# Loading the first gate block as two whole halves, with all three parameter rows moved to GpSimd, in a one-core scan-and-gate kernel

## The chip, the cores and the metric

The kernel runs on one core of one Trainium2 chip. The metric is the device time of one execution in microseconds (us). The kernel before takes 183.2 us, the median of three runs (183.2 to 183.42).

## What is computed

The reference normalises a sequence x of 2048 tokens by 448 channels, and sends the result through two branches. Branch A is a diagonal complex state-space scan over the tokens; branch B is a gated two-layer block whose inner width is 1792. The output is x plus the product of A with silu(B).

```python
x = A_x                                    # (1, 2048, 448) bf16
xn = layernorm(x)
# A: Lam_bar = exp(dt*Lam); h_t = Lam_bar*h_(t-1) + B_bar xn_t ; s = 2 Re(C h) + xn*Dskip
# B: h = sigmoid(xn @ w_gate) * (xn @ w_up) ; b = h @ w_down   (w_gate, w_up: 448 x 1792)
return x + s * silu(b)
```

## The kernel before

The 2048 tokens are cut into 16 tiles of 128 and four chunks (c = 0 to 3) of four tiles. For each chunk TensorE (PE) computes 14 blocks of 128 columns of the gate and of the up product (lines 808 and 809), the projection of branch A (`b_phase`, lines 882 to 899), and later the down product (line 1024) and the output of A (line 1043). ScalarE (ACT) applies tanh to the gate blocks (lines 842 and 839), VectorE (DVE) multiplies by the up blocks (line 845) and runs the scan (line 963), GpSimd (POOL) does small arithmetic, SyncE (SP) issues nearly all DMAs.

A planner, `Plan`, decides the order. Every operation is given to it with an engine, a cost and its reads and writes; `solve` first gives each operation a due time counted back from PE's fixed order, then simulates forward and, on each engine, picks the ready operation that is due first. A DMA's landing is modelled from a rate and, if `land` is given, is not earlier than that. The order that comes out is then issued as it is: each engine works through its own list and waits at the head of it. So the numbers `land` change no transfer, but they decide which instruction stands ahead of which on ACT, DVE and POOL.

PE's product of a block of 128 columns needs two halves of weights, on the lower and the upper 64 partitions (line 808 reads the one, line 809 the other). The gate weights come in three blocks of columns: m = 0 and 1, m = 2 and 3, m = 4 to 6. Before, the first block comes in four pieces, A and B of each half (`load_w0`, lines 374 to 379): piece A holds the row groups that PE's first products on tile 0 read (part "b" of `last_tile`, lines 826 and 827), piece B the rest (part "a"). Three pieces are issued by SP and one by ACT. The three parameter rows (`load_p`, line 400) go one by SP and two by POOL; they are transposed on PE by `columns` (lines 635 and 637), which stands in PE's order between the transposes of tile 0 and the first product. A memset by POOL of two elements of the second gate block (line 418) makes SP's later weight loads wait for POOL. Every DMA on SP or ACT also uses one of eight semaphores in turn, and its issue waits until the DMA eight places earlier has landed.

At the start PE runs ten warming products (line 445), transposes tile 0 (lines 569 and 571), the parameter rows, part "b" of tile 0, the transposes of tile 1 (lines 589 and 590), part "a" of tile 0, then the rest. Tiles 0 to 3 are normalised by DVE (line 531). Tiles 4 to 7 follow for the next chunk: statistics by DVE (lines 451 and 457), a power by POOL (lines 510 and 511), two small operations by DVE (lines 513 and 514, tile `nmr`), then the normalisation by ACT (line 535). Sine and cosine tables are made by DVE (lines 676, 678 and 688) and ACT (lines 669, 681, 683 and 685). Three PSUM tiles `gu` are used in turn by PE's products; u5, the sixth up block of chunk 0, and the second part of `b_phase` of chunk 0 share one of them.

Of the kernel before, what the change touches and what calls it, by code (L numbers as in the profile page):

```python
# [14 lines left out]
ACT = mybir.ActivationFunctionType  # L15
# [3 lines left out]
D = 448  # L19
F = 1792  # L20
P = 128
H = 64
# [51 lines left out]
class Plan:  # L74
# [10 lines left out]
    def add(self, eng, cost, fn, r=(), w=(), dma=0, lat=None, chain=False, name="", rate=230e3):  # L85
        o = Op()
        o.idx, o.eng, o.cost, o.fn, o.dma, o.name = len(self.ops), eng, cost, fn, dma, name
        o.lat = LAT.get(eng, 0.0) if lat is None else lat
        o.pre, o.suc, o.rate = {}, [], rate
        o.slot, o.land = None, 0.0  # L90
        if dma and eng != "POOL":
            o.slot, self.n_dma = self.n_dma, self.n_dma + 1
        o.start = o.end = None
        for k in r:
            if k in self.w:
                self._edge(self.w[k], o, True)
        for k in w:
            for q in self.r.get(k, ()):
                self._edge(q, o, False)
            if k in self.w:  # L100
                self._edge(self.w[k], o, True)
        for k in w:
            self.w[k] = o
            self.r[k] = []
        for k in r:
            if k not in w:
                self.r.setdefault(k, []).append(o)
        if chain or eng == "PE" or (eng in ("DVE", "ACT") and self.seq):
# [138 lines left out]
def kernel(  # L247
# [18 lines left out]
    V, A, G, T, Q = nc.vector, nc.scalar, nc.gpsimd, nc.tensor, nc.sync  # L266
# [17 lines left out]
    wgt = {"g": sbt("wG", [7, 896]), "u": sbt("wU", [7, 896])}  # L284
# [66 lines left out]
    add = pl.add  # L351
# [3 lines left out]
    def load(eng, key, nbytes, o, i, cost=0.45, r=(), rate=230e3, land=0.0):  # L355
        e = {"SP": Q, "ACT": A, "POOL": G}[eng]
        add(eng, cost, lambda: e.dma_start(out=o, in_=i), w=[key] if not isinstance(key, list) else key,  # L357
            r=r, dma=nbytes, chain=True, rate=rate).land = land

    def load_x(t0, n, q="SP", r=(), rate=230e3, land=0.0):  # L360
        load(q, [("x", t) for t in range(t0, t0 + n)], n * P * D * 2,
             x_all[:, t0:t0 + n, :], x_src[:, t0:t0 + n, :], r=r, rate=rate, land=land)
# [8 lines left out]
             wgt[k][ps, :, m0 * P:m1 * P],  # L371
             wsrc[k][:, c0 + m0 * P:c0 + m1 * P].rearrange("(s p) f -> p s f", p=H), cost=0.65, r=r, rate=rate, land=land)

    def load_w0(eng, half, part, r=(), land=0.0):
        ps = slice(half * H, half * H + H)
        s0, c0 = (1 - half if part == "A" else half), half * 896
        n = 4 - s0
        load(eng, [("w", "g", half, m, part) for m in range(2)], H * n * 2 * P * 2, wgt["g"][ps, s0:7:2, 0:2 * P],
             wsrc["g"][:, c0:c0 + 2 * P].rearrange("(s p) f -> p s f", p=H)[:, s0:7:2, :], cost=0.5, r=r, rate=400e3, land=land)

    def wkeys(k, m, part=None):
        if k == "u" or m > 1:
            return [("w", k, 0, m), ("w", k, 1, m)]
        if part == "b":
            return [("w", k, 0, m, "A"), ("w", k, 1, m, "A")]
        return [("w", k, h, m, q) for h in range(2) for q in "AB"]

    def load_wd(h):
        fs = slice(h * 7, h * 7 + 7)
# [11 lines left out]
    def load_p(eng, k, r=()):  # L401
        load(eng, ("vrow", k), D * 2, vrow[k:k + 1, :], (A_log_dt, A_Lambda_im, A_Lambda_re)[k].unsqueeze(0), cost=0.75 if eng == "POOL" else 0.45, r=r)
    load_x(0, 1, "SP")
    load_x(1, 1, "ACT")
    load_x(2, 1, "SP", rate=180e3)
    load_x(3, 1, "ACT", rate=180e3)
    load_p("SP", 2)
    add("ACT", 0.05, lambda: A.preload_act_table_set("sqrt_and_others"), w=["sqrttab"], lat=1.3, chain=True)
    load_w0("SP", 0, "A", land=5.7)
    load_w0("ACT", 1, "A", land=5.9)  # L410
    load_w0("SP", 0, "B", land=6.9)
    load_w0("SP", 1, "B", r=[("x", 1)], land=6.9)
    load_p("POOL", 0)
    load_p("POOL", 1)
    add("POOL", 0.15, lambda: G.memset(ident[:], 0.0), w=["ident"], chain=True)
    add("POOL", 0.4, lambda: G.affine_select(out=ident[:], in_=ident[:], compare_op=ALU.not_equal, fill=1.0, base=0,
                                             pattern=[[-1, P]], channel_multiplier=1), r=["ident"], w=["ident"], chain=True)
    add("POOL", 0.1, lambda: G.memset(wgt["g"][0:1, 0, 256:258], 0.0), w=[("w", "g", 0, m) for m in (2, 3)], chain=True)
    load_w("SP", "g", 0, 1, rate=400e3, land=8.8)
    load_w("SP", "g", 1, 1, rate=400e3, land=9.8)  # L420
    load_w("SP", "g", 0, 2, rate=400e3, land=11.2)
    load_w("SP", "g", 1, 2, rate=400e3, land=12.6)
    load_x(4, 2, land=14.0)
    add("POOL", 0.1, lambda: G.memset(halfc[:], 0.5), w=["consts"])
    add("POOL", 0.1, lambda: G.memset(negc[:], -1.0), r=["consts"], w=["consts"])
    add("POOL", 0.1, lambda: G.memset(expc[:], math.e), w=["expc"])
# [3 lines left out]
                                    allow_small_or_imprecise_dtypes=True), w=[("wv", 0)])  # L430
    add("POOL", 0.15, lambda: G.memset(flat(g_raw[:, 512:2048], 3, 512)[:, :, D:512], 0.0),
        w=[("xnw", t) for t in (1, 2, 3)])
    load_w("SP", "u", 0, 0, rate=400e3, land=15.6)
    load_w("SP", "u", 1, 0, rate=400e3, land=16.8)
    load_x(6, 2, land=17.9)
    load_w("SP", "u", 0, 1, rate=400e3, land=19.0)
    load_w("SP", "u", 1, 1, rate=400e3, land=20.1)
    load_w("SP", "u", 0, 2, rate=400e3, land=21.6)
    load_w("SP", "u", 1, 2, rate=400e3, land=23.1)


    def warm_mm(n, w=512):
# [299 lines left out]

    def b_load():
        for i, m in enumerate((A_B_re, A_B_im)):
            tload([("bT", i)], bT[:, 0:3, i, :], m[:, 0:384], D * 768, land=25.0 + 1.7 * i)
            tload([("bT3", i)], bT[:, 3:4, i, :], m[:, 320:448], D * 256, land=25.7 + 2.0 * i)
# [68 lines left out]
    def last_tile(c, k, steps, j, hs="ba"):  # L815
        x, w_ = xnT[c % 3], wgt[k]
        ts = slice(j * P, j * P + P)
        for h in hs:
            ss = {"a": (0, 2, 4, 6), "b": (1, 3, 5), "c": (0, 2, 4), 1: (6,)}[h]
            for m, a in steps:  # L820
                ms = slice(m * P, m * P + P)

                def f(ms=ms, a=a, ss=ss):
                    for s in ss:
                        go, end = (s == 1, s == 6) if hs[0] == "b" or hs == "a" else (s == 0, s == 5)
                        T.matmul(gu[a][:, 0, ts], lhsT=w_[0:H, s, ms], rhs=x[0:H, SL[s], ts], start=go, stop=end)  # L826
                        T.matmul(gu[a][:, 1, ts], lhsT=w_[H:P, (s + 1) % 7, ms], rhs=x[H:P, SL[s], ts], start=go, stop=end)  # L827
                add("PE", len(ss) * 0.0562, f, r=[("xnT", c % 3, j, "a" if h == "c" else h)] + wkeys(k, m, "b" if h == "b" else "a"), w=[("gu", a)],
                    name=f"{k}{c}.{m}")

    sg_n = [0]
# [227 lines left out]
    def yout(c, j, first=False):  # L1059
        t = c * TPC + j  # L1060
        g, o, q = gt_of[c, j], next_o(), t % NXD
        a = next_acc()
        key, ok, od = ("acc", a), ("o", o, 0), o_t[o][:]
        y = y_mm(c, j, acc[a], key, 0, D, False, first)
        add("DVE", dve1(D), lambda: V.tensor_tensor(out=od, in0=y, in1=xd[q][:], op=ALU.add), r=[key, ("xd", q)], w=[ok])
        add("DVE", dve2(D), lambda: V.tensor_tensor(out=od, in0=od, in1=g_t[g][:], op=ALU.mult), r=[ok, ("gt", g)], w=[ok])
        add("DVE", dve2(D), lambda: V.tensor_tensor(out=od, in0=od, in1=x_all[:, t, :], op=ALU.add), r=[ok, ("x", t)], w=[ok])
        rows = (0, H, P) if c == 2 and j == 3 else (0, P)
        for r0, r1 in zip(rows, rows[1:]):
            store(t, od, 0, D, r0, r1, [ok])  # L1070

# [84 lines left out]
    gu_mm(0, "g", 3, None, 0, TPC, False)  # L1156
    gu_evac(0, "g", 3, None)
    b_load()
    load("SP", "dbc", P * D * 2, dbc[:], A_Dskip.unsqueeze(0).to_broadcast((P, D)), rate=400e3, land=29.0)

    def stats_for(c):
        for t in range(4 * c, 4 * c + 4):
# [103 lines left out]
```

## Time and profile before

| What | Value |
|---|---|
| median of three runs | 183.2 us |
| span of the profiled execution, first to last instruction | 181.5 us |
| granted TensorE clock | 1.000 |
| busy: PE, DVE, ACT, POOL | 177.1, 166.4, 98.2, 37.6 us |
| first four x tiles, issue to landing | 2.4 to 2.9 us |
| first gate block, last piece: issued, landed | 3.47, 7.21 us |
| x tiles 4 and 5: issued, landed | 6.86, about 13.7 us |
| x tiles 6 and 7: issued, landed | 8.84, about 17.3 us |

The profiled execution's own time beside its span is not listed; the median stands 1.7 us over the span, which is what lies around it. "Landed" is the issue's start plus the time to landing that the trace gives for that DMA; for the last piece of the gate block it is the end of its entry in the chain. The profile's engine rows count busy time; a matmul is pipelined, so that a start-to-start distance says more than a duration. Times in the chain and the timeline count from the first instruction.

### The profile page before, as it was taken

The page shows a single profiled execution, that of the slowest core. Times are in us where ns is not written, and L with a number is a line of the kernel's source. Part 1 is how long each engine was busy: PE and PEld are TensorE (multiplying, and loading weights), DVE is VectorE, ACT ScalarE, POOL GpSimd, SP SyncE. Part 2 cuts the span into 40 slices and gives each one's busy share as a digit, 9 for nine tenths or more (in the row PEclk, how much of TensorE's full clock was granted, in tenths as well). Part 3 has the DMA queues.
Part 4 walks back from the last instruction along what each step waited for, and adds up shares of the span by engine and source line. Part 5 has one row for each costly group of instructions (what it writes and reads, how often), then busy time and mean ns, then how long its engine had stood idle before and what let it go on. Part 6 is the DMA issues. An engine that isn't in the chain of part 4 may idle for free.

```text
span 181.5 us, 3611 instructions
## 1 busy us (share of the span) xinstructions
PE 177.1 (98%) x1404; PEld 88.2 (49%) x1411; DVE 166.4 (92%) x294; ACT 98.2 (54%) x162; POOL 37.6 (21%) x94
## 2 busy tenths in 40 slices
PE   8999999999999999999999999999999999999993
PEld 2664445664544444445554444444555444455552
DVE  3778799999989999999999999999999999999772
ACT  5799998857699985364155543348110533411100
POOL 6472468100018797000004100000000000000000
PEclk9999999999999999999999999999999999999999
DMA  5999999999000290000004900002000000002121
GB/s 133 227 224 229 160 165 207 252 242 257 23 0 0 52 148 6 0 4 0 0 2 88 143 0 0 4 0 69 7 4 0 25 27 28 1 0 76 47 65 47
DMA packets 30853, 13.43 MB, mean 74 GB/s; under 512 B 19442, under 2 KB 30835, under 8 KB 30835
## 3 DMA queue, kind: packets, MB, share of 16 engines
q1 hardware_dynamic: 30210, 12.83, 34.9%
q10 hardware_dynamic: 560, 0.36, 0.7%
q8 instruction: 11, 0.18, 0.5%
q14 instruction: 8, 0.06, 0.1%
q0 software_dynamic: 64, 0.00, 0.0%
HBM read 6.77 MB, written 1.84 MB: 47 GB/s over the span
## 4 chain that ended last, share of the span: by engine, by line
PE 94%; DMA 2%; SPq 1%; DVE 1%; issue 0%; DVEq 0%
PE gu L808 43%; PE gu L1024 15%; PE acc L1043 11%; PE acc L1024 9%; PE gu L896 8%; DMA wG<-in_B_w_gate_dram 2%; PE acc L899 2%; PE gu L882 2%; SPq L357 1%; PE gu L826 1%; PE acc L808 1%; PE gu L809 1%; DVE o_t L1085 0%; PE gu L827 0%; DVE o_t L1079 0%
## 5 line engine op out<-in xcount | busy, mean ns | idle before, releaser
L808 PE MATMUL gu<-xnT,wU 64*128 64x512 bf16 x196 | 45.8, 376 | 0.0
L809 PE MATMUL gu<-xnT,wU 64*128 64x512 bf16 x196 | 45.8, 376 | 0.0
L808 PE MATMUL gu<-xnT,wG 64*128 64x512 bf16 (+1 forms) x189 | 41.3, 360 | 0.0
L809 PE MATMUL gu<-xnT,wG 64*128 64x512 bf16 (+1 forms) x189 | 41.3, 360 | 0.0
L842 ACT ACTIVATE sig<-gu 128x1024 f32<-128x1024 f32 x21 | 21.3, 1019 | 24.4 <-PE gu L809 19.8
L1024 PEld LDWEIGHTS <-hF 128*128 128x128 bf16 x224 | 21.9, 98 | 20.6
L808 PEld LDWEIGHTS <-wU 64*128 64x128 bf16 x196 | 18.4, 94 | 22.9
L808 PEld LDWEIGHTS <-wG 64*128 64x128 bf16 x196 | 18.4, 94 | 19.9
L1024 PE MATMUL gu<-wd,hF 128*128 128x448 bf16 x140 | 28.0, 352 | 0.0
L845 DVE SCALAR_TENSOR_TENSOR hF<-sig,gu 128x1024 bf16<-128x1024 f32 x21 | 25.4, 1210 | 0.7 <-ACT sig L842 0.4
L1043 PE MATMUL acc<-cT,hT 128*128 128x448 bf16 (+2 forms) x119 | 22.9, 337 | 0.0
L963 DVE TENSOR_TENSOR_SCAN wv<-c_r,st,z 128x512 bf16<-128x512 f32 x18 | 22.8, 1273 | 0.0
L1030 ACT ACTIVATE g_t<-gu 128x448 bf16<-128x448 f32 x10 | 5.4, 540 | 27.7 <-PE gu L1024 16.8
L809 PEld LDWEIGHTS <-wU 64*128 64x128 bf16 x196 | 18.4, 94 | 0.0
L809 PEld LDWEIGHTS <-wG 64*128 64x128 bf16 x196 | 18.4, 94 | 0.0
L1024 PE MATMUL acc<-wd,hF 128*128 128x448 bf16 x84 | 16.9, 352 | 0.0
L1043 PEld LDWEIGHTS <-hT 128*128 128x128 bf16 x126 | 11.7, 98 | 9.9 <-issue 0.4
L896 PE MATMUL gu<-xnT,bT 128*128 128x512 bf16 x65 | 15.3, 379 | 0.4
L910 ACT CAST bus<-gu 128x1024 bf16<-128x1024 f32 x12 | 12.0, 1011 | 5.9 <-PE gu L882 5.3
L541 POOL COPY xn<-xn 128x448 bf16<-128x448 bf16 x12 | 7.5, 627 | 27.2 <-ACT xn L535 27.0
L916 ACT CAST bus<-acc 64x256 bf16<-64x256 f32 (+1 forms) x24 | 8.7, 368 | 4.8 <-PE acc L899 4.5
L535 ACT ACTIVATE xn<-x_all,nmr,rsd 128x448 bf16<-128x448 bf16 x12 | 8.8, 758 | 3.7 <-DVE xd L546 2.2
(162 smaller groups left out, 263.1 us busy)
## 6 DMA issues: line engine op xcount, KB each, us to landing
wd<-in_B_w_down_dram SPq DMA_DIRECT2D x2, 784.0 KB, 6.6
out_dram<-o_t SPq DMA_DIRECT2D x14, 112.0 KB, 1.7
wU<-in_B_w_up_dram SPq DMA_DIRECT2D x4, 224.0 KB, 8.4
x_all<-in_A_x_dram SPq DMA_DIRECT2D x2, 448.0 KB, 5.0
wG<-in_B_w_gate_dram SPq DMA_DIRECT2D x2, 336.0 KB, 5.4
wU<-in_B_w_up_dram SPq DMA_DIRECT2D x2, 336.0 KB, 8.5
wG<-in_B_w_gate_dram SPq DMA_DIRECT2D x2, 224.0 KB, 4.1
x_all<-in_A_x_dram SPq DMA_DIRECT2D x2, 224.0 KB, 7.7
```

Source lines behind the costliest of these rows:

```text
L535: add("ACT", 0.65, lambda: A.activation(o[:, 0:448], x_all[:, t, :], ACT.Identity, bias=nmr[:, t, :], scale=rsd[:, t, :]), r=[("x", t), (" ...
L541: add("POOL", 0.25 if n == H else 0.6, lambda: G.tensor_copy(out=o[:, D:D + n], in_=o[:, 0:n]), r=[("xn", b)], w=[("xnw", b)])
L808: T.matmul(bank[0][:, ts], lhsT=w_[0:H, s, ms], rhs=x[0:H, SL[s], ts], start=(s == 0), stop=(s == 6))
L809: T.matmul(bank[1][:, ts], lhsT=w_[H:P, (s + 1) % 7, ms], rhs=x[H:P, SL[s], ts], start=(s == 0), stop=(s == 6))
L842: add("ACT", act(1024), lambda: A.activation(th, gu[a][:], ACT.Tanh, scale=0.5), r=[("gu", a)], w=[tk])
L845: add("DVE", dve1(1024), lambda: V.scalar_tensor_tensor(out=ho, in0=th, scalar=1.0, in1=gu[a][:], op0=ALU.add, op1=ALU.mult), r=[("gu", a) ...
L896: T.matmul(gu[slots[pt]][:, i, :], lhsT=bT[:, kt, i, pt * P:pt * P + P], rhs=x[:, kt, :], start=(first and kt == 0), stop=(not first and k ...
L910: add("ACT", act(1024), lambda: A.copy(out=bus[u][:], in_=gu[slots[pt]][:]), r=key(pt), w=[("bus", u)])
L916: add("ACT", 0.36, lambda ns=ns, d=d, q=q, l=l, i=i: A.copy(out=bus[u][d, l, ns], in_=acc[a3[i]][q, 0:256]), r=[("acc", a3[i])] + ([("bus" ...
L963: dve(1.194, lambda k=k: V.tensor_tensor_scan(out=wv[:, k, :], data0=rb, data1=z[:, k, :], initial=(st[pt][:, k, :] if c else 0.0), op0=AL ...
L1024: T.matmul(d, lhsT=hF[c % 2][:, m, h, js], rhs=wd[:, ft, :], start=(ft == 0), stop=(ft == FT - 1))
L1043: T.matmul(y, lhsT=hT[c % 2][:, hm, js], rhs=cT[:, cm, c0:c1], start=(i == 0 and not skip_on_pe), stop=(i == 6))
```

## The change

The first gate block is loaded as two whole halves with the helper that the later blocks use, one half by SP and one by ACT. The third parameter row is issued by POOL, behind the other two. The two-element memset goes, so that SP's list runs x, x, first block, second block, third block, x tiles 4 and 5, the up weights with x tiles 6 and 7 in between. Nearly all `land` numbers of the planner get smaller. The output rows of the four tiles of chunk 2 are each stored in two halves of 64 rows, where only the last of them was.

The order of instructions on PE stays the same. On DVE, the statistics of tiles 4 to 7 move ahead of table operations, and those of tiles 6 and 7 now stand ahead of the `nmr` operation of tiles 4 and 5; the skip rows of two tiles stand ahead of one line-845 operation. On ACT, the normalisation of tile 4 (line 535) now stands ahead of the tanh of the seventh gate block, and those of tiles 5 and 6 ahead of the tanh of the fourth. On POOL, one bias copy of the B matrix stands ahead of the copy of tile 7.

```diff
-    def load_w0(eng, half, part, r=(), land=0.0):
...
-    def wkeys(k, m, part=None):
-        if k == "u" or m > 1:
-            return [("w", k, 0, m), ("w", k, 1, m)]
-        if part == "b":
-            return [("w", k, 0, m, "A"), ("w", k, 1, m, "A")]
-        return [("w", k, h, m, q) for h in range(2) for q in "AB"]
+    def wkeys(k, m):
+        return [("w", k, 0, m), ("w", k, 1, m)]
...
-    load_x(2, 1, "SP", rate=180e3)
-    load_x(3, 1, "ACT", rate=180e3)
-    load_p("SP", 2)
+    load_x(2, 1, "SP", land=3.7)
+    load_x(3, 1, "ACT", land=3.8)
+    load_w("SP", "g", 0, 0, rate=400e3, land=5.4)
     add("ACT", 0.05, lambda: A.preload_act_table_set("sqrt_and_others"), w=["sqrttab"], lat=1.3, chain=True)
-    load_w0("SP", 0, "A", land=5.7)
-    load_w0("ACT", 1, "A", land=5.9)
-    load_w0("SP", 0, "B", land=6.9)
-    load_w0("SP", 1, "B", r=[("x", 1)], land=6.9)
+    load_w("ACT", "g", 1, 0, rate=400e3, land=5.4)
+    load_w("SP", "g", 0, 1, rate=400e3, land=6.7)
+    load_w("SP", "g", 1, 1, rate=400e3, land=7.3)
     load_p("POOL", 0)
     load_p("POOL", 1)
+    load_p("POOL", 2)
...
-    add("POOL", 0.1, lambda: G.memset(wgt["g"][0:1, 0, 256:258], 0.0), w=[("w", "g", 0, m) for m in (2, 3)], chain=True)
-    load_w("SP", "g", 0, 1, rate=400e3, land=8.8)
-    load_w("SP", "g", 1, 1, rate=400e3, land=9.8)
-    load_w("SP", "g", 0, 2, rate=400e3, land=11.2)
-    load_w("SP", "g", 1, 2, rate=400e3, land=12.6)
-    load_x(4, 2, land=14.0)
+    load_w("SP", "g", 0, 2, rate=400e3, land=8.5)
+    load_w("SP", "g", 1, 2, rate=400e3, land=9.9)
+    load_x(4, 2, land=10.9)
...
-    load_x(6, 2, land=17.9)
+    load_x(6, 2, land=14.2)
...
-        rows = (0, H, P) if c == 2 and j == 3 else (0, P)
+        rows = (0, H, P) if c == 2 and j > -1 else (0, P)
```

The `land` numbers of the up weights, of the B matrix and of the skip row are lowered in the same way (the last up half from 23.1 to 19.4).

More of the change, by code (lines that the diff above doesn't have):

```diff
@@ L372, in load_w @@
              wsrc[k][:, c0 + m0 * P:c0 + m1 * P].rearrange("(s p) f -> p s f", p=H), cost=0.65, r=r, rate=rate, land=land)
-    def load_w0(eng, half, part, r=(), land=0.0):
[L375 to L379, printed above, removed]
-    def wkeys(k, m, part=None):
-        if k == "u" or m > 1:
-            return [("w", k, 0, m), ("w", k, 1, m)]
-        if part == "b":
-            return [("w", k, 0, m, "A"), ("w", k, 1, m, "A")]
-        return [("w", k, h, m, q) for h in range(2) for q in "AB"]
+    def wkeys(k, m):
+        return [("w", k, 0, m), ("w", k, 1, m)]
     def load_wd(h):
@@ L432 @@
         w=[("xnw", t) for t in (1, 2, 3)])
-    load_w("SP", "u", 0, 0, rate=400e3, land=15.6)
-    load_w("SP", "u", 1, 0, rate=400e3, land=16.8)
-    load_x(6, 2, land=17.9)
[L436 to L439, printed above, removed]
+    load_w("SP", "u", 0, 0, rate=400e3, land=12.0)
+    load_w("SP", "u", 1, 0, rate=400e3, land=13.0)
+    load_x(6, 2, land=14.2)
+    load_w("SP", "u", 0, 1, rate=400e3, land=15.2)
+    load_w("SP", "u", 1, 1, rate=400e3, land=16.2)
+    load_w("SP", "u", 0, 2, rate=400e3, land=17.8)
+    load_w("SP", "u", 1, 2, rate=400e3, land=19.4)
     def warm_mm(n, w=512):
@@ L744, in b_load @@
         for i, m in enumerate((A_B_re, A_B_im)):
-            tload([("bT", i)], bT[:, 0:3, i, :], m[:, 0:384], D * 768, land=25.0 + 1.7 * i)
-            tload([("bT3", i)], bT[:, 3:4, i, :], m[:, 320:448], D * 256, land=25.7 + 2.0 * i)
+            tload([("bT", i)], bT[:, 0:3, i, :], m[:, 0:384], D * 768, land=22.0 + 2.0 * i)
+            tload([("bT3", i)], bT[:, 3:4, i, :], m[:, 320:448], D * 256, land=22.6 + 2.0 * i)
             add("POOL", 0.7, lambda i=i: G.tensor_copy(out=bT6[:, 0:3, i * H:i * H + H], in_=bT[:, 0:3, i, 384:448]),
@@ L827, in f @@
                         T.matmul(gu[a][:, 1, ts], lhsT=w_[H:P, (s + 1) % 7, ms], rhs=x[H:P, SL[s], ts], start=go, stop=end)
-                add("PE", len(ss) * 0.0562, f, r=[("xnT", c % 3, j, "a" if h == "c" else h)] + wkeys(k, m, "b" if h == "b" else "a"), w=[("gu", a)],
+                add("PE", len(ss) * 0.0562, f, r=[("xnT", c % 3, j, "a" if h == "c" else h)] + wkeys(k, m), w=[("gu", a)],
                     name=f"{k}{c}.{m}")
@@ L1158 @@
     b_load()
-    load("SP", "dbc", P * D * 2, dbc[:], A_Dskip.unsqueeze(0).to_broadcast((P, D)), rate=400e3, land=29.0)
+    load("SP", "dbc", P * D * 2, dbc[:], A_Dskip.unsqueeze(0).to_broadcast((P, D)), rate=400e3, land=26.0)
     def stats_for(c):
```

## The prediction

> **What bounds the kernel.** I read the page first: PE is busy 98% of the span, and the chain that ended last is PE for 94% of it.
>
> ```profile
> span 181.5 us, 3611 instructions
> ...
> PE 177.1 (98%) x1404; PEld 88.2 (49%) x1411; DVE 166.4 (92%) x294; ACT 98.2 (54%) x162; POOL 37.6 (21%) x94
> ...
> PE 94%; DMA 2%; SPq 1%; DVE 1%; issue 0%; DVEq 0%
> ```
>
> The kernel ends when PE ends, plus a tail of DVE and one store. So the change can win only where PE stands still, and it touches PE only in the first 30 us. There the chain, in order of time, runs through SP's issues into one transfer:
>
> ```profile
> 2.02 0.75 SPq L357
> ...
> 2.81 0.61 SPq L357
> ...
> 3.47 3.74 DMA wG<-in_B_w_gate_dram
> ...
> 7.25 0.23 PE gu L827
> ```
>
> The fourth piece of the first gate block, issued at 3.47, lands at 7.21 and lets PE go on. The timeline around it shows how much PE lost:
>
> ```profile
> 6.73 0.22 PE L590 MATMUL gu<-ident,g_t 128*128 128x128 bf16 x1
> ...
> 6.88 0.23 PE L826 MATMUL gu<-xnT,wG 64*128 64x128 bf16 x1
> ...
> 7.25 0.09 PEld L827 LDWEIGHTS <-wG 64*128 64x128 bf16 x1 [0.28 <-DMA wG<-in_B_w_gate_dram]
> ```
>
> Line 827 follows line 826 by 0.37 us; further on the two start together (7.32 and 7.32). So the stall is **0.37 us**, and from 7.25 to the end PE's groups show no idle time but 0.4 us in all at line 896, without a releaser. This is the most the change can give: 0.2% of the time. A difference of 0.2% is also about what a measurement of this kernel can tell from no change.
>
> **What the change does, part by part.**
>
> *The first block.* Now all 448 KB of it must be there for PE's first product (6.11 in the timeline), where before piece A of both halves sufficed (landed 2.02 + 4.0 = 6.0 and 1.69 + 4.2 = 5.9). When does it land? I take the DMA columns of half-microsecond windows (share, then GB/s):
>
> ```profile
> 2.50:3.00 0.50, 0.50 (x3) 0.22 (x2) 0.00 (x0) 0.44 (x1) 0.42 (x3) 1.00 1.03 307
> 3.00:3.50 0.50, 0.50 (x3) 0.15 (x2) 0.39 (x1) 0.22 (x1) 0.50 (x6) 1.00 0.95 288
> 3.50:4.00 0.50, 0.50 (x2) 0.15 (x1) 0.47 (x3) 0.45 (x2) 0.50 (x4) 1.00 0.58 106
> 4.00:4.50 0.50, 0.50 (x2) 0.15 (x1) 0.50 (x2) 0.44 (x2) 0.06 (x2) 1.00 0.76 171
> ...
> 5.50:6.00 0.50, 0.50 (x10) 0.33 (x7) 0.43 (x4) 0.44 (x3) 0.00 (x0) 1.00 0.56 125
> ```
>
> Until 3.5 the windows have moved (84+242+307+288) x 0.5 = 460 kB, which is the four x tiles (4 x 112 KB). Then the engines run half empty, because the pieces were issued late. In the changed kernel SP issues its half right behind x (at 1.64, where the parameter row stood, some 0.65 each) and ACT at 1.69, both done by 2.4. The remaining 459 kB then go from 3.5 on, at a rate between 177 GB/s (mean of the six windows 3.5 to 6.5) and 297 (mean of 2.5 to 3.5): 1.55 to 2.6 us. To landing I add 0.6 (the fourth x tile landed at 1.19 + 2.9 = 4.1 with its bytes moved by 3.5). That is 5.65 to 6.7. I take **5.65**, since both queues will be loaded as in 2.5 to 3.5, the nearest row. Then PE starts at 6.11 as before, held by ACT's copy of tile 0, and the stall is gone: **-0.37**. Landing at 6.7 would start PE at 6.75, and part "a" 0.77 later (6.88 - 6.11) at 7.52 instead of 7.25: +0.27. Break-even is 6.45.
>
> Behind the stall, what is late next? The transposes of tile 3 need DVE's normalisation, ending at 6.88 + 0.40 = 7.28; moved 0.37 forward they start at 7.67. Part "b" of tile 1 needs a DVE copy ending at 8.21; PE reaches it near 8.42. Both hold. The second gate block is needed at 10.34 instead of 10.71 and landed at 4.84 + 4.3 = 9.1; it now comes earlier.
>
> A rule of the Trainium skill speaks against one half of the idea: DMA: Bandwidth & Descriptors, section "Issuing engines are not separate DMA queues", says that DMAs from several engines share the same 16 DMA engines, and that a second issuing engine saves only issue time. The windows agree: 277 to 300 GB/s at 6.5 to 7.5, with SP's queue alone, against 288 to 307 with both. By it the gain is from the earlier issue alone, which is how the sum counts it.
>
> *The parameter rows.* POOL's two rows were issued at 1.25 and 2.02 and took 3.0 and 2.9 us. The third follows at 2.53 and lands near 5.45 (bounds: 4.9, where the second landed, and 6.0, with another half us of crowding). `columns` on PE starts at 5.69 and has about 0.05 us of cover before part "b" at 6.11, so cost 0, or up to 0.3 at the late end. POOL's setup moves 0.5 us later: `epsc` ends at 3.7, needed by ACT at 4.06; the rest ends near 4.6, and POOL was idle until 5.10. The memset saves 0.1 there.
>
> *ACT, DVE and the x tiles.* Here a new bound stands. ACT's list is dense from 8.2 to 30 us, and PE's `b_phase` hangs on it:
>
> ```profile
> 25.14 0.61 ACT L683 ACTIVATE spm<-hT 128x512 bf16<-128x512 f32 x1
> ...
> 25.79 0.68 DVE L688 TENSOR_SCALAR spm<-spm 128x512 bf16<-128x512 bf16 x1
> ...
> 27.72 2.55 DVE L845 SCALAR_TENSOR_TENSOR hF<-hF,gu 128x1024 bf16<-128x1024 bf16 x2
> ...
> 28.84 0.59 PE L882 MATMUL gu<-xnT,bT 64*128 64x512 bf16 x4
> ```
>
> The sine table ends at 25.75 on ACT, DVE takes it at 25.79 and works without a break until u5 is out at about 28.95; the second pair of line 882 needs that PSUM tile at about 29.05. So PE can come forward there only as far as ACT does, plus 0.08. How far does ACT come? Its scaling at 9.19 waits for POOL (8.71 + 0.23), so it gains 0.14 only; the tanh of the sixth block at 16.96 waited for PE 0.12 and starts at 16.70; the next item is free at 17.62. One idle of 0.15 (before 21.83) falls away too. From there to 25.14 is the same work in another order, so the table starts at 24.71: 0.43 earlier, which with 0.08 covers 0.37. But the next item is now tile 4's normalisation, which waits for `nmr` of tiles 4 and 5, and that waits on DVE behind the statistics of tiles 6 and 7. From the landing of x 6 and 7 it is 1.35 us of statistics (17.58 to 18.93 before), and about 0.55 for lines 513, 676 and 514: landing + 1.9. (DVE is free for them by then: x 4 and 5 at 12.2, and 3.2 of statistics and table work behind them.) On time means a landing by **15.7**; each us later costs PE a us. Before it landed at 17.3. All loads keep their order, so they ride on the first block: if that is done 7.21 - 5.65 = 1.55 us earlier, x 6 and 7 land at 15.8. The bound there is 0.51 - 0.1 = 0.41, and 0.37 passes. The other end (first block at 6.7) puts them at 16.8: 0.51 - 1.1 = -0.6.
>
> *The stores.* Three more issues for SP, of 0.33 to 0.6 us, between items it waits for (61.8 us of waiting for line 1067). A half took 2.7 us to land against 1.7; output tile (3,1) is written at 173.08, and its buffer's last half would be issued near 169.5 and land near 172.2. Cost 0; if late, DVE's 1.55 us of idleness before 177.63 covers it.
>
> **Sum.** 181.5 - 0.37 = 181.1 of span, and with 1.7 around it 182.85; the median shown is 183.2, so I predict **182.85 us**.
>
> **Rivals.**
> 1. *The x tiles hold ACT* (slower). DVE's statistics of tiles 6 and 7 now stand ahead of what ACT waits for. It decides above a landing of 16.2, where ACT's 0.51 is spent. For it: landings before lagged further behind with every load. Against: SP issues those tiles some 2 us earlier. At 16.8: 183.8; at the old 17.3: 184.3. Chance 0.18.
> 2. *The block lands between 6.1 and 6.45, or x between 15.8 and 16.2*: the stall is partly kept, 182.9 to 183.3. Chance 0.20.
> 3. *The block or the third row lands late*, since all of it is now needed at once and POOL's row shares the engines with more traffic: block at 6.7, 183.5; row at 6.0, 0.3 lost of 0.37, 183.1. For it: the slow windows from 3.5 may be the transfers' own start, not late issue. Chance 0.12.
>
> **How the numbers follow.** Forecast 0.50, with its own range 182.75 to 182.95: the limit of 0.37 lies just at the 0.2% (182.83), so about half of it counts as faster. Faster: 0.26. Slower by over 0.2% (above 183.57): rival 1 nearly whole and some of 3, 0.25. Within: 0.49. Range: 182.7 to 183.8 leaves out the worse part of rival 1 and little else.
>
> **What would show it.** Right: no idle before line 827 of old, PE's first 512-column product at about 10.35 instead of 10.71, the second pair of `b_phase` near 28.7. Wrong: an idle on PE before part "b" named after wG or the row; ACT idle before tile 4's normalisation near 17.6 with DVE waiting for x; PE idle at about 29 behind DVE.

## The result, and the profile after

The changed kernel takes **185.07 us** (median of six executions, 183.97 to 186.63) against 183.2 (182.94 to 183.42) beside it on the same chip: a ratio of 1.0114, 95% interval 1.0072 to 1.0157. It is slower by 1.9 us between the medians; the ratio, here and below, is that of the means. The six fall into two groups: three at 183.97 to 184.37, with a granted TensorE clock of 1.000, and three at 185.77 to 186.63, with 0.988 to 0.991. The median lies between the two. The profiled execution is of the first group: 184.29 us, span 182.5.

The page of the changed kernel: the tensor engine (PE) is as busy as before, and the chain that ended last is still nearly all PE, but its DMA share rose from 2% to 3%.

```profile
span 182.5 us, 3621 instructions
...
PE 94%; DMA 3%; DVE 1%; ACTq 0%; issue 0%; ACT 0%; DVEq 0%
```

The chain of work in order of time (start, duration, what) now has ScalarE's (ACT's) half of the first gate block where SyncE's (SP's) fourth piece stood:

```profile
0.73 0.41 ACTq L357
1.17 0.46 ACTq L357
1.69 5.71 DMA wG<-in_B_w_gate_dram
```

That half was issued 1.8 us earlier than the piece that PE waited for before, and it landed at 1.69 + 5.71 = 7.40, 0.2 us later than that piece (7.21). The timeline of PE (start, duration, instruction, idle time before it and what ended it) shows what this did. Lines 621 and 623 are `columns`, lines 812 and 813 part "b" of tile 0, lines 826 and 827 of before:

```profile
6.24 0.21 PE L621 MATMUL acc<-ident,hF 3*128 3x3 bf16 x3 [0.15 <-DMA hF<-in_A_Lambda_re_dram]
6.38 0.19 PE L623 MATMUL acc<-ident,hF 3*64 3x3 bf16 x2
6.95 0.23 PE L812 MATMUL gu<-xnT,wG 64*128 64x128 bf16 x1 [0.38 <-DMA wG<-in_B_w_gate_dram]
7.45 0.23 PE L813 MATMUL gu<-xnT,wG 64*128 64x128 bf16 x1 [0.27 <-DMA wG<-in_B_w_gate_dram]
```

Before, part "b" began at 6.11, since it needs only the two A pieces, and PE stood 0.37 us later, at part "a". Now part "b" needs both halves entire and runs at 7.45. PE's first product of 512 columns, before and after:

```profile
10.71 0.38 PE L808 MATMUL gu<-xnT,wG 64*128 64x512 bf16 x1
```
```profile
11.67 0.38 PE L794 MATMUL gu<-xnT,wG 64*128 64x512 bf16 x1
```

It is 0.96 us late, and the span is 1.0 longer. The windows of the changed kernel (stretch; busy time of PE, PEld, DVE, ACT, POOL; granted clock; DMA share; GB/s) show the transfers:

```profile
2.50:3.00 0.50, 0.50 (x3) 0.23 (x2) 0.00 (x0) 0.44 (x1) 0.50 (x3) 1.00 1.10 368
...
3.50:4.00 0.50, 0.50 (x2) 0.15 (x1) 0.47 (x3) 0.50 (x2) 0.50 (x5) 1.00 0.35 38
4.00:4.50 0.50, 0.50 (x2) 0.15 (x1) 0.50 (x2) 0.39 (x3) 0.50 (x4) 1.00 0.31 45
4.50:5.00 0.50, 0.50 (x2) 0.00 (x0) 0.50 (x4) 0.50 (x2) 0.01 (x1) 1.00 0.87 213
5.00:5.50 0.50, 0.50 (x5) 0.34 (x5) 0.50 (x2) 0.47 (x4) 0.24 (x1) 1.00 1.15 331
```

Both halves were issued by 2.4, and yet the hole behind the x tiles, 3.5 to 4.5, is deeper than before (38 and 45 GB/s; before 106 and 171). Of the block's 896 packets of 512 bytes, 65 had started by 4.5. From 5.0 on the DMA engines are loaded again (331 GB/s), but not with the first block alone: SP issued the second block from 2.4 on.

### The profile page after: what moved, and what is told of

It is laid out like the page before. It is cut to its first block, busy times and chain, and to the rows that moved or that the text cites. A ratio compares the mean times of both kernels' runs of the same rounds, so it can differ in the third digit from the quotient of the medians.

```text
span 182.5 us, 3621 instructions
## 1 busy us (share of the span) xinstructions
PE 177.8 (97%) x1411; PEld 88.8 (49%) x1411; DVE 165.6 (91%) x294; ACT 98.2 (54%) x162; POOL 36.9 (20%) x94
## 4 chain that ended last, share of the span: by engine, by line
PE 94%; DMA 3%; DVE 1%; ACTq 0%; issue 0%; ACT 0%; DVEq 0%
PE gu L794 43%; PE gu L1010 15%; PE acc L1029 11%; PE acc L1010 9%; PE gu L882 9%; DMA wG<-in_B_w_gate_dram 3%; PE acc L885 2%; PE gu L868 2%; PE gu L812 2%; PE gu L795 1%; PE acc L794 1%; ACTq L357 0%; DVE o_t L1071 0%; PE gu L813 0%; DVE o_t L1065 0%; PE acc L575 0%
## 5 line engine op out<-in xcount | busy, mean ns | idle before, releaser
L882 PE MATMUL gu<-xnT,bT 128*128 128x512 bf16 x72 | 16.7, 379 | 0.0
L437 DVE BATCH_NORM_STATS2 bst<-x_all 128x6 f32<-128x448 bf16 x11 | 6.4, 613 | 5.0 <-DMA x_all<-in_A_x_dram 5.0
```

Of the source, the lines that this page charges most:

```text
L437: add("DVE", 0.56 if t < TPC else 0.6, lambda: V.bn_stats(out=bst[b][:], in_=x_all[:, t, :]), r=[("x", t)] + ([("xnT", 0, 3, "a")] if 3 < ...
L882: T.matmul(gu[slots[pt]][:, i, :], lhsT=bT[:, kt, i, pt * P:pt * P + P], rhs=x[:, kt, :], start=(first and kt == 0), stop=(not first and k ...
```

## The experiments

Each kernel is one of the two with an edit, given as a diff. The kernel before was run again beside every group: 183.01 to 183.24 us.

**The parts, one at a time.** First the block alone, on the kernel before (the pieces and their keys gone, all else as it was):

```diff
-    load_w0("SP", 0, "A", land=5.7)
-    load_w0("ACT", 1, "A", land=5.9)
-    load_w0("SP", 0, "B", land=6.9)
-    load_w0("SP", 1, "B", r=[("x", 1)], land=6.9)
+    load_w("SP", "g", 0, 0, rate=400e3, land=5.7)
+    load_w("ACT", "g", 1, 0, rate=400e3, land=5.7)
```

> The kernel before, with one part of the change alone: the first gate block in two whole halves, one issued by SP and one by ACT; parameter row, memset and planner numbers as before. Theory (block): two whole halves deliver late because the first products need all 448 KB, and the data begin to flow only near 4.5 us; the block lands at 7.2 to 7.5, PE waits ahead of part b of tile 0, and the run is 0.5 to 1.0 us slower, with some runs at a mean clock near 0.99 and 2 us slower still. Rival (row): the block by itself lands near 5.7 to 6.3 as I forecast, and the time is within 0.3 us of before or faster. Rival (order): no change, since the later order on ACT and DVE is not in it.

Measured: 184.96 (184.17 to 186.35), ratio 1.0108 (1.0070 to 1.0146). The block alone gives the whole loss, with both of its groups: three executions at 184.17 to 184.26 with a clock of 1.000, three at 185.65 to 186.35 with 0.991. Its profiled execution is of the second group. PE stood 1.33 us for the block, and some time later its clock fell:

```profile
7.16 0.23 PE L820 MATMUL gu<-xnT,wG 64*128 64x128 bf16 x1 [1.33 <-DMA wG<-in_B_w_gate_dram]
```
```profile
6.00:7.00 1.00, 0.00 (x0) 0.00 (x0) 0.93 (x5) 0.60 (x3) 0.24 (x1) 1.00 1.20 197
8.00:10.00 2.00, 2.00 (x31) 1.61 (x32) 0.61 (x2) 1.19 (x3) 1.74 (x8) 0.53 1.11 227
10.00:12.00 2.00, 2.00 (x52) 2.00 (x48) 1.82 (x6) 1.98 (x4) 0.92 (x3) 0.61 1.13 231
```

Read the column behind POOL's: 0.53 and 0.61 of the clock in two stretches of 2 us in which PE is busy throughout. That is 2 x (1 - 0.53) + 2 x (1 - 0.61) = 1.7 us of PE's work lost, and the two groups lie 1.4 to 2.2 us apart. Cut finer, the windows show a clock of 0.50 from 8.14 to 11.55 and of 1.00 on both sides.

Next the third row alone:

```diff
-    load_p("SP", 2)
     load_p("POOL", 1)
+    load_p("POOL", 2)
```

> The kernel before, with one part alone: the third parameter row issued by GpSimd behind the other two. Theory (block): the row lands near 6.1 as in the changed kernel, PE waits for it up to 0.4 us, but the last piece of the block at 7.2 hides that; within 0.3 us of before. Rival (row): GpSimd's third transfer takes the DMA engines' time at 3.5 to 4.5, all four pieces land 0.5 us or more later, and the run is 0.5 us or more slower.

Measured: 183.22 (182.93 to 183.52), ratio 1.0004 (0.9996 to 1.0013): nothing. PE's stall of 0.37 at part "a" is gone in its trace, since SP's pieces are 0.38 earlier, and the first product of 512 columns comes at 10.37, 0.34 earlier. This is all that the change set out to win, and half of it is gone again at 29 us: line 899 of `b_phase` starts at 29.29 instead of 29.48. The span is 181.4 against 181.5, and the time doesn't show it.

Then all the rest, with block and row as before: the new due times, no memset, the last stores in halves.

```diff
-    add("POOL", 0.1, lambda: G.memset(wgt["g"][0:1, 0, 256:258], 0.0), w=[("w", "g", 0, m) for m in (2, 3)], chain=True)
-    load_w("SP", "g", 0, 1, rate=400e3, land=8.8)
+    load_w("SP", "g", 0, 1, rate=400e3, land=6.7)
...
-        rows = (0, H, P) if c == 2 and j == 3 else (0, P)
+        rows = (0, H, P) if c == 2 and j > -1 else (0, P)
```

> The kernel before, with all the rest of the change: no memset, the later landing numbers of the planner (and so the new order on ACT, DVE and POOL), output rows of chunk 2 stored in halves; first block and row as before. Theory (block): within 0.3 us of before, x tiles 6 and 7 landing near 17. Rival (order): statistics of x tiles 6 and 7 hold the normalisation on ACT, PE waits at about 29 us, 0.5 to 1.1 us slower.

Measured: 184.64 (184.09 to 185.06), ratio 1.0078 (1.0062 to 1.0095). This part loses too, by itself, which the loss of the block had not let one expect. Its chain of waits leaves PE between 8.8 and 30:

```profile
8.79 9.06 DMA x_all<-in_A_x_dram
17.88 1.15 DVE bst L450 x2
```

and ACT's timeline shows why. Line 534 normalises tile 4 and stands at the head of ACT's list:

```profile
15.38 2.17 ACT L841 ACTIVATE hF<-gu 128x1024 bf16<-128x1024 f32 x2
19.73 0.76 ACT L534 ACTIVATE xn<-x_all,nmr,rsd 128x448 bf16<-128x448 bf16 x1 [2.17 <-DVE nmr L513]
```

The planner, told of earlier landings, put tile 4's normalisation ahead of the tanh operations that stood before it. It needs `nmr` of tiles 4 and 5, and on VectorE (DVE) that stands behind the statistics of x tiles 6 and 7. It did so before too, but there ACT came to the normalisation (line 535) long after `nmr` (line 514) was ready:

```profile
17.58 1.13 DVE L451 BATCH_NORM_STATS2 bst<-x_all 128x6 f32<-128x448 bf16 x2
18.84 0.13 DVE L514 SCALAR_TENSOR_TENSOR nmr<-mv,rsd 128x2 f32<-128x2 bf16 x1
```
```profile
18.83 1.04 ACT L842 ACTIVATE hF<-gu 128x1024 bf16<-128x1024 f32 x1
19.73 1.43 ACT L535 ACTIVATE xn<-x_all,nmr,rsd 128x448 bf16<-128x448 bf16 x2
```

(What is new on DVE is that line 513 of tiles 4 and 5 moved behind those statistics; line 514 was there already.) In this kernel tiles 6 and 7 landed at 17.85, so ACT stood 2.17 us, and PE stood twice behind it (0.80 us start to start near 20.7, 1.19 near 29). To see whether the order alone does it, the due times were changed and nothing else:

```diff
-    load_w("SP", "g", 0, 1, rate=400e3, land=8.8)
+    load_w("SP", "g", 0, 1, rate=400e3, land=6.7)
...
-    load_x(6, 2, land=17.9)
+    load_x(6, 2, land=14.2)
...
```

> The kernel before with one edit: the due times given to the planner for the loads after the first block (and with them the order in which ScalarE and VectorE take their work) are those of the changed kernel; the first block, the third row, the memset and the stores are those of before. In the run of all the remaining edits ScalarE stood 2.17 us before tile 4's normalisation for VectorE's nmr, which hung on x tiles 6 and 7 landing at 17.85. Theory 1 (the order alone does it): the same two waits, 184.3 to 185.0 us, with the tensor engine idle near 20.7 and 29. Theory 2 (the missing memset or the halved stores did it): 183.1, with no idle time of the tensor engine after 8 us.

Measured: 183.85 (183.80 to 184.81), ratio 1.0048 (1.0031 to 1.0065). The wait is there, and goes with the landing: here x 6 and 7 landed at 17.27, 0.58 earlier, tile 4's normalisation started at 19.13, 0.60 earlier, ACT stood 1.24 instead of 2.17, and PE once, near 29 (0.83 start to start). The median is below what was expected, whose price was taken from the later landing. Transfers, loads and their order are those of before: an order alone costs 0.6 us by the medians and 0.9 by the means, since three of the seven executions lie at 184.40 to 184.81.

**Is the low clock a cost of its own?** In two kernels PE was given further warming products, in a buffer that is overwritten, where it stood: four in the changed kernel,

```diff
...
+        def fill():
+            for _ in range(4):
+                T.matmul(gu[u2][:, 1, :], lhsT=ones[:, 0:P], rhs=ones[:, 0:512], start=True, stop=True)
+        add("PE", 0.001, fill, w=[uk[1]])
         last_tile(0, "g", steps01, 0, "b")
```

> The changed kernel, with four more warming products of 512 columns on PE between the parameter rows and part b of tile 0, into a half of a PSUM tile that nobody reads; they add about 0.85 us of work where PE waits for the block. Theory (clock): the spread of the changed kernel, 184.0 to 186.6 at mean clocks of 1.0 to 0.988, comes from PE standing idle for 0.9 us near 6.5 to 7.4; filled, the clock stays at 1.0 in every run and the times lie at 184.0 to 184.5. Rival: the spread comes from the block landing at varying times; the times still reach 186 and the clock still falls.

and six, in the same place, in the kernel that has only the whole block:

> The kernel before with the block as two whole halves, and six further warming products of 512 columns (0.213 us each at the full clock, 1.28 us in all; they write a buffer that is overwritten, so the output is the same) where the tensor engine stood 1.5 us for the block. The block itself lands no earlier. Theory 1 (two costs: the late block, about 1.0 us in every execution, and half a clock for some microseconds after the idle time in some of them): the executions of 185.6 to 186.4 go, all lie at 184.1 to 184.5, and the granted clock from 8 to 12 us is 1.00. Theory 2 (the low clock has nothing to do with the idle time): the executions near 186 stay. Theory 3 (only the clock costs, the lateness is covered): 183.2.

Measured: 184.87 (184.49 to 184.94) and 184.32 (184.19 to 184.70). In both the executions near 186 are gone: none of nine. In the first the products came behind a wait of 1.00 us for the third row and cost some time themselves, so the median fell little. The second is the clean one: the kernel without them had 184.17 to 184.26 where the clock was full and 185.65 to 186.35 where it wasn't; with them nothing is above 184.70, and the windows have a full clock where that one had 0.53 and 0.61:

```profile
8.00:10.00 2.00, 2.00 (x58) 1.78 (x58) 0.95 (x4) 1.58 (x4) 1.74 (x8) 1.00 1.11 229
10.00:12.00 2.00, 2.00 (x66) 1.76 (x62) 1.87 (x6) 1.98 (x4) 0.95 (x3) 1.00 1.14 238
```

So the late block costs about 1.1 us in every execution, and the idle time that it makes costs some 1.7 us more in about half of them.

**Why is the block late?** Three kernels start from the changed one. The first cuts the block in pieces again, two on each queue:

```diff
-    load_w("SP", "g", 0, 0, rate=400e3, land=5.4)
+    load_w0("SP", 0, "A", land=5.4)
+    load_w0("SP", 0, "B", land=5.4)
-    load_w("ACT", "g", 1, 0, rate=400e3, land=5.4)
+    load_w0("ACT", 1, "A", land=5.4)
+    load_w0("ACT", 1, "B", land=5.4)
```

> The changed kernel with its first block cut into the four pieces of before, the two of each half on that half's own queue (SyncE the one, ScalarE the other); rows, order, later loads and stores as changed. Theory 1 (the loss is that part b of the last tile, which needs only the odd pieces, now waits for the whole block): part b starts by 6.2 us, the tensor engine's idle time before it falls under 0.5 us, no low clock, 183.0 to 183.6 us. Theory 2 (the bytes come late whatever the cut, since the later loads share the engines): the even pieces land past 7.2 and the time stays at 184.0 or above.

Measured: 185.54 (184.76 to 186.52), ratio 1.0111 (1.0089 to 1.0134). What theory 1 forecast for the time did not come. Part "b" did start early (6.48), but ACT's second piece came 1.3 us later than the whole half had, and part "a" waited for it:

```profile
7.26 0.23 PE L825 MATMUL gu<-xnT,wG 64*128 64x128 bf16 x1
8.71 0.28 PE L826 MATMUL gu<-xnT,wG 64*128 64x128 bf16 x1 [1.22 <-DMA wG<-in_B_w_gate_dram]
```

The packets of ACT's queue tell where it went. By 5.5 us 263 of its 448 packets of 512 bytes had started; between 5.5 and 6.5 only 85 followed, while SP's queue, which was in the second block by then, started 274. But this is no clean test of the cut: ACT issued its second piece only at 3.38 (the whole half at 1.69), behind the second block's first half, which SP issued at 3.08.

The second kernel holds the second block back by a copy that POOL makes once x tile 3 is there:

```diff
+    add("POOL", 0.1, lambda: G.tensor_copy(out=wgt["g"][0:1, 0, 256:258], in_=x_all[0:1, 3, 0:2]), r=[("x", 3)],
+        w=[("w", "g", 0, m) for m in (2, 3)], chain=True)
     load_w("SP", "g", 0, 1, rate=400e3, land=6.7)
```

> The changed kernel with the second gate block, and all that SyncE issues behind it, held back until GpSimd has read a word of x tile 3 (landed near 4.1), so that the first block has the DMA engines to itself. All later loads move by some 2 us too, x tiles 6 and 7 to past 18, which by the order's price costs up to 2 us near 29: the total is not the reading here, the landing of the block is. Theory 1 (the second block's packets hold the first up): the first block lands by 6.6 and the tensor engine's product of the gate begins at least 0.5 us earlier than in the changed kernel (7.45). Theory 2 (a whole half is slow to start, however empty the engines): the hole from 3.5 to 4.5 us stays and the block lands past 7.2.

Measured: 186.22 (185.31 to 187.55), slower as expected from the later x tiles (PE stood 1.61 and 1.39 us start to start near 29), and the reading is the block's landing. From issue to landing, SP's half and ACT's half (the issues of 1.5 to 2.6 us; last column, median us to landing):

```profile
wG<-in_B_w_gate_dram SPq DMA_DIRECT2D x1, 224.0 KB, 4.6
wG<-in_B_w_gate_dram ACTq DMA_DIRECT2D x1, 224.0 KB, 4.9
```

The block is there at 1.69 + 4.9 = 6.6 instead of 7.40, and PE doesn't wait for it at all (part "b" starts at 6.80, right behind `columns`, which stood behind ACT and POOL here). So with nothing issued behind it the block was there 0.8 us earlier, in the one profiled execution of each kernel. The size is not sharp: in the five profiled kernels that issue the second block right behind the whole halves (at 2.4 to 3.2), the block landed at 7.05 to 7.95. The hole remains in part: 111 and 192 GB/s in 3.5 to 4.0 and 4.0 to 4.5, with one weight transfer a queue outstanding. By 4.5 us 323 packets of weights had started, against 65 in the changed kernel. At the 331 GB/s of 5.0 to 5.5 those 258 packets are 0.4 us, so by this estimate about half of the 0.8 arises in the hole, and the rest once both blocks move. ACT's queue carries no weights but its half, so that its last packet can be told: it started at 6.70 in the changed kernel and at 5.91 here, 0.7 us ahead of the landing in both. The half was late because its packets started late, not because its landing was reported late.

The third kernel asks whether two queues make the mixing:

```diff
-    load_w("ACT", "g", 1, 0, rate=400e3, land=5.4)
+    load_w("SP", "g", 1, 0, rate=400e3, land=5.4)
```

> The changed kernel with both whole halves of the first block issued by SyncE, one behind the other and ahead of the second block. Theory 1 (in the changed kernel ScalarE's half shares the engines with the second block, which SyncE issues from its own queue 0.7 us later; behind one another in one queue the first block goes first): both halves land by 6.9, the tensor engine's first product of the gate starts by 7.1 instead of 7.45 for the second half, and the time falls to 183.4 to 184.1 us with no execution near 186. Theory 2 (one queue is half as fast as two, so that is what matters): the block lands past 7.4 and the time is 184.5 us or more. Theory 3 (a whole half is slow whatever its neighbours): as the changed kernel, 184.0 to 186.6.

Measured: 185.62 (183.98 to 186.28, five executions; a sixth, at 187.06, isn't in these figures), ratio 1.0111 (1.0070 to 1.0151): as the changed kernel, with two executions at 184.0 and three from 185.6 on. Theory 1 fell. The first half came at 6.38, the second no earlier than in two queues:

```profile
6.38 0.23 PE L812 MATMUL gu<-xnT,wG 64*128 64x128 bf16 x1 [0.19 <-DMA wG<-in_B_w_gate_dram]
7.37 0.28 PE L813 MATMUL gu<-xnT,wG 64*128 64x128 bf16 x1 [0.76 <-DMA wG<-in_B_w_gate_dram]
```

In SP's queue 896 packets of weights, as many as the block has, had started by 5.75; yet its second half counted as landed at 2.42 + 4.90 = 7.32. Either some of the block's packets went behind the second block's, or the landing is reported only when what follows has moved on; in one queue the records don't tell the two apart. The Trainium skill (DMA: Bandwidth & Descriptors, section "Queues, rings and completion order") says that a queue is 16 rings, one on each DMA engine, and that the write which reports completion waits for all earlier writes of that engine, across its queues. That rule speaks of earlier writes, so by itself it doesn't say why loads issued later in the same queue should delay the 7.3; no run tests it. The same section says that an engine takes turns between the queues it has work for, packet by packet: between 5.0 and 6.0 us of the changed kernel, ACT's queue started 312 packets and SP's 327, which agrees.

**What undoes the loss?** Three more start from the changed kernel. With the first block as before (four pieces, three on SP, ahead of the second block) and all else as changed:

```diff
-    load_w("SP", "g", 0, 0, rate=400e3, land=5.4)
-    load_w("ACT", "g", 1, 0, rate=400e3, land=5.4)
+    load_w0("SP", 0, "A", land=5.4)
+    load_w0("ACT", 1, "A", land=5.4)
+    load_w0("SP", 0, "B", land=6.5)
+    load_w0("SP", 1, "B", r=[("x", 1)], land=6.5)
```

> The changed kernel with its first block loaded as before (four pieces, ScalarE one of them, SyncE the other three ahead of the second block); rows, order, missing memset and stores as changed. Theory 1 (two losses, of which the late block hid the other): the tensor engine's first product of 512 columns comes at 10.3 to 10.7 instead of 11.67, but near 29 it now stands for VectorE, since x tiles 6 and 7 land at 16.5 to 17.5 and the new order has ScalarE wait for them: 183.4 to 184.6 us. Theory 2 (the block is the whole loss): 182.8 to 183.3 us and no idle time near 29.

Measured: 184.63 (183.94 to 185.30), ratio 1.0084 (1.0061 to 1.0107). The block is in time (PE doesn't wait for it), and now the order costs what it costs by itself: in the profiled execution, the fastest of the six, x 6 and 7 land at 8.38 + 8.59 = 16.97, ACT stands 1.18 us, and PE 0.77 start to start near 29.

```profile
18.85 0.76 ACT L534 ACTIVATE xn<-x_all,nmr,rsd 128x448 bf16<-128x448 bf16 x1 [1.18 <-DVE nmr L513]
```

The block's last piece, issued at 3.07, landed at 6.45, so the whole block was there earlier than any whole-half block with loads right behind it. The same holds for the other three kernels with four pieces, three of them on SP, and the row on POOL (the row alone, and the two below): 6.4 to 6.5, with the second block issued from 3.7 on. Whether the cut or the later second block does this was not separated.

With the due times of before as well:

```diff
-    load_w("SP", "g", 0, 1, rate=400e3, land=6.7)
+    load_w("SP", "g", 0, 1, rate=400e3, land=8.8)
...
-    load_x(6, 2, land=14.2)
+    load_x(6, 2, land=17.9)
...
```

> The changed kernel with both suspects undone: the first block as before, and the due times of before for the later loads. What is left of the change is the third row on GpSimd, the missing memset and the last stores in halves. Theory 1 (the block and the order are the whole loss): 182.9 to 183.3 us, within 0.1% of the run with the row alone (183.22). Theory 2 (the missing memset or the stores cost too): above 183.5 us.

Measured: 183.44 (183.16 to 183.86), ratio 1.0019 (1.0008 to 1.0029). Most of the loss is gone, and 0.4 us stay against the kernel before in the same group (183.06). That lies between the bands of the two theories. The trace places these 0.4 at the very end. PE's first product of 512 columns comes at 10.26, 0.45 earlier than before, and DVE's last operation ends at 178.80 instead of 179.04. But from there to the end of the span it is 2.88 us, against 2.50 before, and SP waits 1.2 us for the last store at its last line, against 0.8. All five profiled kernels that have both the four pieces and the stores in halves show it (2.80 to 2.88), and none of the nine others (2.49 to 2.61). Those five are all the rest of the change, the pieces on two queues, and the last three; so 0.3 to 0.4 us of their profiled executions belongs neither to the block nor to the order. Why the end is longer was not tried.

Last, the kernel with the block undone, and x tiles 6 and 7 asked for ahead of the first block of the second weight:

```diff
+    load_x(6, 2, land=14.2)
-    load_w("SP", "u", 0, 0, rate=400e3, land=12.0)
-    load_w("SP", "u", 1, 0, rate=400e3, land=13.0)
-    load_x(6, 2, land=14.2)
+    load_w("SP", "u", 0, 0, rate=400e3, land=14.2)
+    load_w("SP", "u", 1, 0, rate=400e3, land=14.8)
```

> The run with the block undone (e10: rows, new order, stores as changed, first block as before), with one more edit: x tiles 6 and 7 are asked for before the first block of the second weight instead of behind it, some 1.3 us earlier. Theory 1 (what e10 lost near 29 us was ScalarE, in the new order, waiting for these tiles): they land by 15.6, ScalarE's idle time before tile 4's normalisation (17.7 in before) is under 0.3 us, the tensor engine doesn't stand near 29, and the time falls from 184.63 to 182.8 to 183.4 us. Theory 2 (the new order loses for another reason): the tensor engine still stands 0.7 us there, 183.9 us or more. Theory 3 (the weights, now later, hold the tensor engine up near 18 us, where it first needs them): a new wait there, named after the second weight.

Measured: 183.57 (183.27 to 183.91), ratio 1.0025 (1.0014 to 1.0037): 1.06 us better than without this edit. No wait for the second weight appeared, so theory 3 is out. Theory 1 was right in part: the tiles landed at 14.65 and the time fell, but it missed its bands. ACT still stands 0.85 us and PE 0.63 start to start near 29, since DVE now works without a break from 13.8 to 18.0, at the statistics of tiles 4 to 7 and table work between them, behind x 4 and 5, which landed only at 6.42 + 7.34 = 13.76. The profiled executions of the two kernels lie only 0.16 apart (183.94 and 183.78); why the others of the kernel without the edit are slower than its profiled one isn't shown. No kernel of this study is faster than the one before.

## Why the prediction was wrong, step by step

*The first block, landing at 5.65.* This step failed, and the sum with it: measured 7.40. The bytes were right, and the rate was reached, only later: 297 GB/s was forecast, and from 5.0 to 6.5 the engines moved 324 to 333. Two other terms failed. The flow was to start at 3.5, since the hole from 3.5 to 4.5 was taken for late issue; but the hole is still there with both halves issued by 2.4, and 65 of 896 packets had started by 4.5. And all that moved was to be the block's own: by 6.0 us 910 packets of weights had started, more than the block has, but ACT's half had 396 of its 448. Held clear of later loads the block lands at 6.6, within the bounds given (5.65 to 6.7), at their far end. With the second block issued behind it, it lands outside them. The sum had no term for the loads that follow, though the same edit brings these forward.

*PE starts at 6.11 as before.* It followed from the landing and fell with it. The rule that the prediction gave for a late landing held: PE starts 0.05 behind it, part "a" comes 0.77 later, against 7.25 before. For 7.40 that is 7.45 + 0.77 - 7.25 = 0.97 us; measured 0.96. The four pieces had hidden these 0.77 us of PE's work while the rest came. Whole halves take that cover away, and so a landing only 0.2 us later than before costs almost five times as much.

*The gain, -0.37.* Not borne out even where the stall is gone. With the row alone PE is 0.34 earlier at 10 us and 0.19 at 29, and the time is that of before.

*Rival 3, the block lands late.* It had the right place, and even a reason that fits the hole ("the slow windows from 3.5 may be the transfers' own start"), but a chance of 0.12 and a price of 0.27 at its end. Measured: 1.1 us.

*The clock.* Not in the prediction at all; PE's idle time was counted at its own length. A sign of it stood in the trace of before: its ten warming products of 512 columns take 4.43 us, 0.43 to 0.44 each, and products as wide take 0.22 start to start from 10.71 on.

```profile
0.77 4.43 PE L445 MATMUL gu<-const-bfloat16-1.0 128*128 128x512 bf16 x10 [0.77 <-PEq L1250]
```

The windows give a clock of 1.00 for that stretch, so the sign stands in the durations alone.

*The third row.* The cost of 0 holds by itself (183.22). In the changed kernel the row landed at 6.1 against 5.45 forecast, at the late bound, and PE stood for it, but the block came later still, so it cost nothing there.

*ACT, DVE and the x tiles.* The mechanism of rival 1 was right, and so were its numbers for ACT: the normalisation starts 1.9 us behind the landing in three traces (17.85 and 19.73, 17.27 and 19.13, 16.97 and 18.85). One detail was wrong: the statistics of tiles 6 and 7 don't "now stand" ahead of what ACT waits for, they did before; ACT now asks earlier. Two figures on the way were off. The landing of these tiles doesn't ride on the first block: the block was 0.2 us later than before, and the tiles came at 16.2, 1.1 earlier. And x 4 and 5, put at 12.2, landed at 13.35 in the changed kernel and at 13.76 where DVE's work behind them became the limit. The point of decision was given as 16.2; in the changed kernel the tiles landed just there, with PE 0.96 us late besides, so the wait is not in its trace. That is chance. It shows in every run that has the new order and the block in time: 184.64, 183.85, 184.63, 183.57.

*The stores.* Cost 0 was forecast. In the changed kernel the end of the span is as long as before (2.50 us behind DVE's last operation); with the four pieces and the stores in halves together it is 0.3 to 0.4 longer, a term that the sum didn't have.

The two losses don't add. The late block alone makes 184.96, the order with the block in time 184.63 (0.3 to 0.4 of it at the end of the span), both together 185.07: the one hides the other.

## What to carry to other kernels

A transfer that PE waits for is not late by its bytes alone: count what is issued behind it until it lands, since that delayed the landing by 0.8 us in the one comparison made here, and weigh it against what holding the rest back costs (here more than it won). Cutting a load along the order in which its consumer reads it hid more here than issuing it earlier in one piece, as long as no piece stood behind the next block. An edit can also win its stall and not the time: follow the gain to the next wait. And due times that are too hopeful cost an in-order engine just as a real delay would, so set them from the landings that a profile shows.

## What was not expected of the hardware

- An idle time of the tensor engine of only 1.3 us (5.83 to 7.16) was followed by a granted clock of 0.53 and 0.61 in 8 to 10 and 10 to 12 us, in about half of the executions. The Trainium skill (TensorE: Matmul & The Clock Gate, section "What's actually happening") has the clock halved after an idle window of about 3.4 us. In the three profiled executions that show the low clock (block alone, pieces on two queues, one queue) it was 0.50 for 3.41 us each time: 8.14 to 11.55, 8.40 to 11.81 and 7.41 to 10.82. That fits a window of that length and costs 1.7 us, but far less idle time was enough. In the one-queue kernel the longest wait was 0.76 us; with four filling products behind a wait of 1.00 us, none of four executions showed it. Whether the clock fell varied from one execution to the next.
- The hole of about 1 us behind the x tiles is not filled by issuing more transfers early: 106 and 171 GB/s with pieces, 111 and 192 with one whole half a queue and nothing behind, 49 and 104 in the kernel with the block alone, 38 and 45 in the changed kernel. In one queue it was 76 and 188, with as much issued. Why was not settled.
- Between 5.7 and 6.0 us as many packets had started as the block has, in four kernels with whole halves (changed, block alone, held back, one queue), and the block landed at 6.6 with nothing behind it and at 7.1 to 7.4 with the second block behind.
